# Linear attention and two mixture layers on one core: denominators on ScalarE, the first item in two single banks, numerators ahead of keys-values, and one decode step on GpSimd

## The chip, the cores and the metric

The kernel runs on one core of one Trainium2 chip. The metric is device time in microseconds (us), from the launch of the program to its end. Before the change it took 1583.85 us (median of 3 runs, 1583.15 to 1584.65).

The engines are named as the profile names them: PE is TensorE (PEld its weight loads, which overlap the matmuls), DVE is VectorE, ACT is ScalarE, POOL is GpSimd, SP is SyncE, which issues most DMAs. SBUF is the on-chip memory, PSUM the eight accumulator banks of 128 partitions x 512 fp32 that PE writes.

## The reference, cut to what matters

Three stages follow each other; the change lies in the first, and in the preparation of weights for the second.

```
# attention: q, k, v are (8, 8, 576, 64); w_phi is (64, 128)
proj = x @ w_phi;  proj -= max(abs(proj), axis=-1)
phi  = concat(exp(proj), exp(-proj))                    # 256 features, for q and for k
kv   = k_p^T v          (256 x 64 per head)
z    = sum over the sequence of k_p
num  = q_p @ kv;  den = q_p . z + 1e-6;  out = num / den
# second stage: h = x @ w_in; g = h * cos(h); g @ w_out      (4608 tokens, 512 -> 2048 -> 512)
# third stage: top-1 routing to 8 experts, relu MLP of each  (512 -> 1024 -> 512)
```

The weights of the second stage arrive as 64-bit floats and are decoded to fp32 on the chip.

## The kernel before, in words

**Attention** (`attention`, lines 46 to 326) works on 16 items, each a pair of batches and a pair of heads. An item has 9 blocks of 128 rows, in five groups `g` of 2, 2, 1, 2 and 2 blocks. `step(j,m)` (line 288) is one step of the steady state: it does one part of several items at once, so that the engines have independent work. An item of time is five steps, m = 0 to 4; m = 2 handles the group of one block and is about half as long. In a step, in this order:

- `proj` (line 151): PE multiplies the transposed q rows by `w_phi` into the PSUM tile `pj` and the transposed k rows into `pjk`. For each DVE then takes the maximum of the absolute values (L161) and subtracts it (L162), which gives `t_q` and `t_k`. So four DVE instructions a step.
- `outT` (line 250): PE transposes the finished rows `xs` of an earlier group into a free half of `pjk`, and ACT copies them to `xo` (L258).
- `qexp` (line 211): PE transposes `t_q` into the PSUM tile `tr`, ACT takes two exponentials, of plus and minus (L225).
- `turn` (line 133): PE transposes raw rows of a later item, ACT copies them (L143, L147).
- `kv` (line 185): PE accumulates keys-values into the PSUM tile `kv`, from the k exponentials `ke`; `kvfin` (line 204) copies the finished sums to SBUF on ACT (L208).
- `num` (line 229): PE multiplies the q exponentials by these sums into the PSUM tile `pn`, whose last column of each block is the denominator. DVE adds 1e-6 (L245), takes the reciprocal (L246) and multiplies (L247), which gives `xs`. `pn` is one bank, so the next numerators wait until L247 has read it.
- `kexp` (line 176): ACT takes the two k exponentials (L181).

The first item has no item before it to hide behind. `begin(m)` (line 271) drives it: its transposes go whole (`whole`, line 128) into the two halves of the one PSUM tile `tr`, and its projections alternate between `pj` and `pjk`, q and k in the same tile, with `by_bank` (line 165) for the second group.

**The weight decode** (`begin`, `decodes`, `decode_part`, lines 449 to 488) turns one 128 x 512 weight block in seven instructions: an absolute value on ACT (L459), then on DVE a minimum (L460), a shift (L461) and two bit-wise merges (L462, L463), a copy on ACT (L464) and a subtraction (L465). 21 blocks are decoded beside the attention, one instruction or two in each step, between the steps; the other 11 in the first part of the second stage. DVE and ACT keep the order in which the program writes these instructions (`pinned`, `keep`), and so does PE in the attention. The driver is at lines 918 to 933.

**The second and third stage** (`moes`, line 387) follow. `route1` (line 625) copies token numbers into `rec` with a DVE instruction that the scheduler may place (L648).

Of the kernel before, what the change touches and what calls it, by code (L numbers as in the profile page):

```python
# [11 lines left out]
F32 = mybir.dt.float32  # L12
# [8 lines left out]
P = 128  # L21
# [24 lines left out]
def attention(tc, ctx, S, ident, q, k, v, w_phi, xt):  # L46
# [7 lines left out]
    pp=pctx.enter_context(tc.tile_pool(name="a_ps",bufs=1,space=PSUM))  # L54
    pk=ctx.enter_context(tc.tile_pool(name="a_kv",bufs=1,space=PSUM,side="right"))
    pj,pjk=(pp.tile([P,2,512],F32,tag=n,name=n) for n in ("pj","pjk"))
    tr=pk.tile([P,2,512],F32,tag="tr",name="tr")
    flat=itertools.count()

    w2=ap.tile([P,F],F32,name="w2",bufs=1)  # L60
    for i in range(2): tc.keep_in_program_order(nc.scalar.dma_start(w2[i*D:(i+1)*D,:],w_phi))
    nc.scalar.preload_act_table_set("natural_log_exp_and_others")

    items=[(bp,hp) for bp in range(4) for hp in range(4)]
    NI=len(items)
# [57 lines left out]
    def over(dst,c,src):  # L123

        for r in range(2): keep(nc.tensor.transpose(dst[:,r,c*H:(c+1)*H],src[r*H:(r+1)*H],ident[r*H:(r+1)*H,r*H:(r+1)*H]))
    def got(dst,a,c): return dst[:,:,a*H:c*H].rearrange("p r (c t) -> p c r t",t=H)
    def like(x): return x.rearrange("p (c r t) -> p c r t",r=2,t=H)
    def whole(srcs):

        pt=tr[:,next(flat)%2,:]  # L130
        for c,x in enumerate(srcs): keep(nc.tensor.transpose(pt[:,c*P:(c+1)*P],x,ident))
        return pt
    def turn(i,m,pt=None,base=0):
# [14 lines left out]
        return vec  # L148

    ts={}  # L150
    def proj(i,g,t,out,o=0):
        c0,n=GR[g]
        x=T[t,i]
        for c in range(n):
            for s in range(2):
                keep(nc.tensor.matmul(out[:,s,o+c*F:o+(c+1)*F],x[s*D:(s+1)*D,(c0+c)*P:(c0+c+1)*P],w2[s*D:(s+1)*D,:],start=True,stop=True))  # L156
        tt=ts[t,i,g]=S(t+"t",f"t_{t}_{i}_{g}")
        def vec():
            gg=out[:,:,o:o+n*F].rearrange("p s (c f) -> p s c f",f=F)
            m=ap.tile([P,4],F32,tag=t+"m",name=f"m_{t}_{i}_{g}")[:,:2*n].rearrange("p (s c) -> p s c",s=2)  # L160
            keep(nc.vector.tensor_reduce(m,gg,AX.X,ALU.max,apply_absolute_value=True))  # L161
            keep(nc.vector.tensor_tensor(tt[:,:n*256].rearrange("p (s c f) -> p s c f",s=2,f=F),gg,  # L162
                m.unsqueeze(3).to_broadcast([P,2,n,F]),ALU.subtract))
        return vec
    def by_bank(i,g,out):
        ms=[]
        for s in range(2):
            ms.append(ap.tile([P,4],F32,tag="qk"[s]+"m",name=f"m_{s}_{i}_{g}"))
            keep(nc.vector.tensor_reduce(ms[s],out[:,s,:].rearrange("p (c f) -> p c f",f=F),AX.X,ALU.max,apply_absolute_value=True))
        for o,t in ((0,"q"),(1,"k")):  # L170
            for s in range(2):
                keep(nc.vector.tensor_tensor(ts[t,i,g][:,s*256:(s+1)*256].rearrange("p (c f) -> p c f",f=F),out[:,s,o*256:(o+1)*256].rearrange("p (c f) -> p c f",f=F),
                    ms[s][:,2*o:2*o+2].unsqueeze(2).to_broadcast([P,2,F]),ALU.subtract))
# [37 lines left out]
    def qexp(i,g):  # L211

        n=GR[g][1]; tt=ts.pop(("q",i,g))
        srcs=[tt[:,(s*n+c)*F:(s*n+c+1)*F] for c in range(n) for s in range(2)]
        w=2*n*P
        x=ap.tile([P,1024],F32,tag="qx",name=f"qx_{i}_{g}",bufs=4)
        qx[i,g]=x[:,:2*w].rearrange("p (k h c) -> p k h c",h=2,k=2)
        if i==0 and g<3:
            pt=whole(srcs)
            made=[(x[:,kk*w:(kk+1)*w],pt[:,:w]) for kk in range(2)]  # L220
        else:
            for c,y in enumerate(srcs): over(tr,4+c,y)
            made=[(like(x[:,kk*w:(kk+1)*w]),got(tr,4,4+2*n)) for kk in range(2)]
        def vec():
            for (o,p),sign in zip(made,(1.0,-1.0)): keep(nc.scalar.activation(o,p,AF.Exp,scale=sign))  # L225
        return vec

    xss={}; xos={}
    def num(i,g):

        n=GR[g][1]; t0=GR[g][0]
        x=qx.pop((i,g))
        pn=pk.tile([P,512],F32,tag="pn",name=f"pn_{i}_{g}")
        for t in range(n):
            for h in range(2):
                o=pn[:,(2*t+h)*E1:(2*t+h+1)*E1]
                for sg in range(2):
                    for c in range(2):
                        bb=c if t0+t==4 else int(t0+t>4)
                        keep(nc.tensor.matmul(o[64*c:64*c+64],x[:,sg,h,t*P+64*c:t*P+64*c+64],kvs[i,bb][:,2*h+sg,:],start=sg==0,stop=sg==1,skip_group_check=True))  # L240
        pv=pn[:,:2*n*E1].rearrange("p (g d) -> p g d",d=E1)
        xs=xss[i,g]=ap.tile([P,256],F32,tag="xs",name=f"xs_{i}_{g}",bufs=2)
        def vec():
            r=ap.tile([P,4,1],F32,tag="rd",name=f"rd_{i}_{g}")[:,:2*n,:]
            keep(nc.vector.tensor_scalar(r,pv[:,:,D:E1],1e-6,None,op0=ALU.add))  # L245
            keep(nc.vector.reciprocal(r,r))  # L246
            keep(nc.vector.tensor_tensor(xs[:,:n*P].rearrange("p (g d) -> p g d",d=D),pv[:,:,0:D],r.to_broadcast([P,2*n,D]),ALU.mult))  # L247
        return vec

    def outT(i,g):  # L250

        t0,n=GR[g]
        if g==0: xos[i]=ap.tile([P,9*P],F32,tag="xo",name=f"xo_{i}")
        xo=xos[i]; xs=xss.pop((i,g))
        po,base=(pjk,4) if (i,g)<(NI-1,0) else (tr,2*(g%2))
        for t in range(n): over(po,base+t,xs[:,t*P:(t+1)*P])
        def vec():
            keep(nc.scalar.copy(like(xo[:,t0*P:(t0+n)*P]),got(po,base,base+n)))  # L258
# [12 lines left out]
    def begin(m):  # L271

        for i,n in FIRST[m]: turn(i,n)()
        if m>1:
            kexp(0,m-2); qexp(0,m-2)()
        loads(0,m)
        yield
        if m==4: vecs=[proj(0,m,"q",pj),proj(0,m,"k",pjk)]
        else:
            out=(pj,pjk)[m%2]  # L280
            vecs=[proj(0,m,"q",out),proj(0,m,"k",out,256)]
            if m==1: vecs=[lambda: by_bank(0,m,out)]
        if m<1: warm(3)
        if m>1: kv(0,m-2)
        for f in vecs: f()
        if m==4: kvfin(0,0)
        yield
    def step(j,m):

        vecs=[]; dve=[]  # L290
        i,g=at(j,m-2); oi,og=at(j-1,m-2); ki,kg=at(j,m-1)
        if j<NI: dve.append(proj(j,m,"q",pj))
        if oi>=0: vecs.append(outT(oi,og))
        if j<NI: dve.append(proj(j,m,"k",pjk))
        two=j==1 and m==0
        if two: vecs+=[lambda: kexp(0,3),turn(2,0,pjk,4)]
        if i<NI: last=qexp(i,g)
        if two: vecs.append(turn(1,4,tr))
        elif j+1<NI: vecs.append(turn(j+1,m,tr))
        if i<NI: vecs.append(last)  # L300
        for f in vecs+dve: f()
        loads(j,m)
        yield
        if i<NI: kv(i,g)
        last=num(j-1,m)
        if i<NI and g in (2,4): kvfin(i,g//4)
        if ki<NI: kexp(ki,kg)
        last()
        if j==NI-1 and m==4: pctx.close()
        if j==NI and m==1: keep(nc.scalar.preload_act_table(AF.Sin))  # L310
        yield
# [75 lines left out]
def moes(tc, ctx, consts, S, ident, att, end_att, xt, w_in, w_out, x1d, tab, wgt, w1, w2, out):  # L387
# [61 lines left out]
    def begin():  # L449
# [7 lines left out]
        h,l=pair(wtag[which][f],f"w{which}_{f}")  # L457
        (win,wout)[which][f]=(h,l)
        return [lambda: pinned(nc.scalar.activation(t,H.bitcast(F32),AF.Abs,scale=2.0**-112)),  # L459
            lambda: pinned(nc.vector.tensor_scalar(t,t,F32_MAX,None,op0=ALU.min)),  # L460
            lambda: pinned(nc.vector.tensor_scalar(ti,ti,3,None,op0=ALU.logical_shift_left)),  # L461
            lambda: pinned(nc.vector.scalar_tensor_tensor(ti,L,29,ti,op0=ALU.logical_shift_right,op1=ALU.bitwise_or)),  # L462
            lambda: pinned(nc.vector.scalar_tensor_tensor(ti,H,-0x80000000,ti,op0=ALU.bitwise_and,op1=ALU.bitwise_or)),  # L463
# [1 line left out]
            lambda eng: eng.tensor_tensor(l,t,f32(h),ALU.subtract)]  # L465
    def decodes(n):

        d=begin(); yield d[0]()
        for k in range(n):
            d[1](); yield d[2]()  # L470
            yield d[3]()
            d[4](); old=d
            if k+1<n:
                d=begin(); d[0]()
            yield
            pinned(old[5]()); stage(); old[6](nc.gpsimd)
# [148 lines left out]
    def route1(u):  # L625
# [496 lines left out]
```

## Time and profile before

| | us |
|---|---|
| median of 3 runs | 1583.85 |
| the profiled execution | 1583.64 |
| its span, first to last instruction | 1581.9 |
| PE busy in it | 1550.4 (98%) |
| DVE busy in it | 1113.6 (70%) |
| ACT busy in it | 880.6 (56%) |
| POOL busy in it | 397.0 (25%) |

The span has two parts with different limits. The attention takes about the first 320 us; the second stage follows without a gap, then the third. The clock that the throttle granted to PE is at full speed throughout (the page's row PEclk shows 9, 90% or more, in each slice). Row DVE of the page's 40 slices shows 9 in the slices of the attention and 5 to 7 behind it.

### The profile page before, as it was taken

To read this page: it belongs to the slowest core of one execution; us is meant where nothing else is said; L and a number is where in the kernel's file an instruction comes from. 1 tells how busy PE (TensorE), PEld (TensorE's weight loads), DVE (VectorE), ACT (ScalarE), POOL (GpSimd) and SP (SyncE) were. 2 spreads that over 40 slices of the span, in tenths; PEclk is the share of its full clock that TensorE was granted. 3 is DMA by queue.
4 is the path that set the end of the run, shared out by engine and by line. 5 is a ranking of instruction groups with operands and counts; after the bars stand their busy time and mean duration, and the time that the engine had idled before them with its cause. 6 is when DMAs were issued, how large, how long until landed. Compare 5 with 4: busy or idle time off the path is not lost.

```text
span 1581.9 us, 35508 instructions
## 1 busy us (share of the span) xinstructions
PE 1550.4 (98%) x14065; PEld 1339.4 (85%) x14065; DVE 1113.6 (70%) x2303; ACT 880.6 (56%) x1627; POOL 397.0 (25%) x356
## 2 busy tenths in 40 slices
PE   8899999999999999999999999999999999999998
PEld 6889898878888888888888888888899899889986
DVE  6999999968657667675767677655776656565656
ACT  6788788766434344343534344344756656565656
POOL 1111110120223433333433433334122111211212
PEclk9999999999999999999999999999999999999999
DMA  7756555233200001010101001004748667766652
GB/s 213 210 159 172 157 167 156 94 111 95 92 14 24 25 13 41 14 40 8 40 14 41 14 9 39 8 15 152 257 147 323 228 225 255 247 227 220 239 197 86
DMA packets 140850, 189.33 MB, mean 120 GB/s; under 512 B 63015, under 2 KB 87719, under 8 KB 140674
## 3 DMA queue, kind: packets, MB, share of 16 engines
q1 hardware_dynamic: 132754, 166.11, 33.6%
q0 software_dynamic: 7760, 20.79, 3.8%
q8 instruction: 113, 1.85, 0.5%
q14 instruction: 63, 0.52, 0.1%
q10 hardware_dynamic: 160, 0.07, 0.0%
HBM read 155.88 MB, written 31.82 MB: 119 GB/s over the span
## 4 chain that ended last, share of the span: by engine, by line
PE 82%; DVE 12%; DMA 4%; issue 2%; ACT 0%; SPq 0%; POOLq 0%; DVEq 0%
PE ph L517 25%; PE acc L557 19%; PE mh L825 12%; PE po L837 11%; PE acc L562 6%; DMA xg<-x1d,mrec 2%; PE kv L201 2%; DVE t_q L162 2%; DVE t_k L162 2%; DVE m_q L161 2%; DVE m_k L161 2%; PE pn L240 2%; DVE xs L247 1%; PE pjk L156 1%; PE px L807 1%
## 5 line engine op out<-in xcount | busy, mean ns | idle before, releaser
L517 PE MATMUL ph<-x,w 128*128 128x512 f32 x1728 | 418.6, 391 | 2.2 <-DVE fr L539 1.6
L517 PEld LDWEIGHTS ph<-x,w 128*128 128x128 f32 x1728 | 322.7, 188 | 70.3 <-DVE fr L539 2.0
L546 POOL TENSOR_TENSOR gl<-fr,gh 128x512 fp32r<-128x512 f32 x130 | 194.8, 1501 | 433.5 <-DVE gh L545 386.1
L780 DVE TENSOR_TENSOR m<-raw,m 128x512 fp32r<-128x512 f32 x320 | 208.2, 687 | 101.1 <-ACT m L779 73.6
L557 PE MATMUL acc<-w,gh 128*128 128x512 f32 x896 | 275.8, 389 | 0.0
L530 ACT ACTIVATE n<-ph 128x512 int32<-128x512 f32 x144 | 86.0, 597 | 272.5 <-PE ph L517 272.4
L779 ACT CAST m<-raw 128x512 fp32r<-128x512 f32 x320 | 188.1, 619 | 39.5 <-PE mh L825 32.4
L825 PE MATMUL mh<-xT,m 128*128 128x256 f32 x1728 | 201.0, 277 | 0.0
L532 DVE SCALAR_TENSOR_TENSOR fr<-ph,n 128x512 f32<-128x512 f32 x144 | 99.2, 689 | 141.9 <-ACT n L530 127.9
L825 PEld LDWEIGHTS mh<-xT,m 128*128 128x128 f32 x1728 | 197.7, 188 | 1.1 <-DVE m L780 0.8
L557 PEld LDWEIGHTS acc<-w,gh 128*128 128x128 f32 x896 | 168.2, 188 | 34.9
L837 PE MATMUL po<-m,hh 128*128 128x512 f32 x576 | 179.6, 393 | 0.0
L593 DVE SCALAR_TENSOR_TENSOR junk<-x1T,wg 128x512 f32<-128x512 f32 x224 | 179.4, 801 | 0.0
L557 PE MATMUL acc<-w,gl 128*128 128x512 f32 x448 | 174.3, 389 | 0.0
L535 ACT ACTIVATE fr<-fr 128x512 f32<-128x512 f32 x144 | 91.1, 633 | 118.1 <-DVE fr L532 118.0
L539 DVE SCALAR_TENSOR_TENSOR fr<-fr,ph 128x512 f32<-128x512 f32 x144 | 98.7, 685 | 79.7 <-ACT fr L537 79.6
L837 PEld LDWEIGHTS po<-m,hh 128*128 128x128 f32 x576 | 105.2, 188 | 19.7
L837 PE MATMUL po<-m,hl 128*128 128x512 f32 x288 | 112.4, 390 | 0.0
L886 POOL DMA_INDIRECT out_dram<-o,mrec x38 | 43.3, 1139 | 266.2 <-ACT o L885 251.9
L557 PEld LDWEIGHTS acc<-w,gl 128*128 128x128 f32 x448 | 84.1, 188 | 17.5
L201 PE MATMUL kv<-v,ke 128*64 128x65 f32 x2560 | 93.3, 225 | 0.9 <-issue 0.9
L537 ACT ACTIVATE fr<-fr 128x512 f32<-128x512 f32 x143 | 90.4, 632 | 4.3
(244 smaller groups left out, 2262.3 us busy)
## 6 DMA issues: line engine op xcount, KB each, us to landing
raw<-in_moe_w_dram SPq DMA_DIRECT2D x160, 512.0 KB, 5.8
xt<-xo SPq DMA_DIRECT2D x16, 576.0 KB, 3.7
xr<-xt SPq DMA_DIRECT2D x36, 256.0 KB, 2.9
raw_q<-in_q_dram SPq DMA_DIRECT2D x32, 256.0 KB, 4.2
raw_k<-in_k_dram SPq DMA_DIRECT2D x32, 256.0 KB, 3.8
st<-in_moe_w_in_dram SPq DMA_DIRECT2D x16, 512.0 KB, 4.2
st<-in_moe_w_out_dram SPq DMA_DIRECT2D x16, 512.0 KB, 3.7
v<-in_v_dram SPq DMA_DIRECT2D x62, 128.0 KB, 4.5
```

The source lines that it names most:

```text
L201: keep(nc.tensor.matmul(o[f0:f0+64],e[:,col+f0:col+f0+64],vh[:,h,9 if cc==4 and bb else cc,:],start=start,stop=cc==(4,8)[bb],skip_group_ch ...
L517: nc.tensor.matmul(ph,A[:,ws],xhl[u,d][k],start=n[0]==0,stop=n[0]==11); n[0]+=1
L532: ins=nc.vector.scalar_tensor_tensor(g,ph,INV2PI,n,op0=ALU.mult,op1=ALU.subtract)
L539: out0[0]=nc.vector.scalar_tensor_tensor(g,g,-0.5,ph,op0=ALU.add,op1=ALU.mult)
L546: nc.gpsimd.tensor_tensor(gl,g,f32(gh),ALU.subtract)
L557: nc.tensor.matmul(accs[u][c],A[:,ws],B,start=(f==0 and k==0),stop=(f==NF-1 and k==2))
L562: nc.tensor.matmul(accs[u][d],A[:,ws],B,start=(f==0 and k==0),stop=(f==NF-1 and k==2))
L593: return lambda: tc.keep_in_program_order(nc.vector.scalar_tensor_tensor(junk,x1T[u,c],1.0,wg[e],op0=ALU.mult,op1=ALU.mult,accum_out=lgs[u ...
L779: keep(nc.scalar.copy(h,a))
L780: keep(nc.vector.tensor_tensor(l,a,f32(h),ALU.subtract))
L825: nc.tensor.matmul(ph[:,f2*T:(f2+1)*T],A[:,ws],B[d//2][:,xs],start=n==0,stop=n==11); n+=1
L837: nc.tensor.matmul(po[c],A[:,ws],B,start=(f==0 and j==0),stop=(f==NF2-1 and j==2))
```

## The change

Five edits, all of them in the attention and in the decode:

- The first item's whole transposes and its q exponentials use two tiles of one bank each, in a pool of their own (`a_first`), which is closed after `begin`; the tile `tr` of the steady state is made only then. Its projections go q into `pj` and k into `pjk`, as in the steady state; `by_bank` is gone.
- The addition of 1e-6 to the denominators is an ACT instruction (an identity with a bias from the small SBUF tile `eps`), and writes `rd` from PSUM to SBUF. It stands between the two q exponentials of a step, which are now issued separately (`half(0)`, `half(1)`).
- In a step `num` stands ahead of `kv`, and `kvfin` behind the k exponentials.
- The decode's minimum is a GpSimd instruction; DVE begins with the shift.
- The copy of token numbers in `route1` keeps its place in the program. One more group of the last-but-one item's output goes through `tr`.

```
+    first=ExitStack()
+    ps=first.enter_context(tc.tile_pool(name="a_first",bufs=2,space=PSUM,side="right"))
+    tr=[]
...
+    eps=ap.tile([P,1],F32,name="eps",bufs=1)
+    nc.gpsimd.memset(eps,1e-6)
...
-        pt=tr[:,next(flat)%2,:]
+        pt=ps.tile([P,512],F32,tag="tr",name="flat")
...
-        def vec():
-            for (o,p),sign in zip(made,(1.0,-1.0)): keep(nc.scalar.activation(o,p,AF.Exp,scale=sign))
-        return vec
+        def half(kk): keep(nc.scalar.activation(*made[kk],AF.Exp,scale=(1.0,-1.0)[kk]))
+        return half
...
+        r=ap.tile([P,4,1],F32,tag="rd",name=f"rd_{i}_{g}")[:,:2*n,:]
+        keep(nc.scalar.activation(r,pv[:,:,D:E1],AF.Identity,bias=eps))
         def vec():
-            r=ap.tile([P,4,1],F32,tag="rd",name=f"rd_{i}_{g}")[:,:2*n,:]
-            keep(nc.vector.tensor_scalar(r,pv[:,:,D:E1],1e-6,None,op0=ALU.add))
             keep(nc.vector.reciprocal(r,r))
...
-        po,base=(pjk,4) if (i,g)<(NI-1,0) else (tr,2*(g%2))
+        po,base=(pjk,4) if (i,g)<(NI-2,3) else (tr[0],2*(g%2))
...
     def begin(m):
         for i,n in FIRST[m]: turn(i,n)()
         if m>1:
-            kexp(0,m-2); qexp(0,m-2)()
+            half=qexp(0,m-2)
+            kexp(0,m-2); half(0); half(1)
         loads(0,m)
         yield
-        if m==4: vecs=[proj(0,m,"q",pj),proj(0,m,"k",pjk)]
-        else:
-            out=(pj,pjk)[m%2]
-            vecs=[proj(0,m,"q",out),proj(0,m,"k",out,256)]
-            if m==1: vecs=[lambda: by_bank(0,m,out)]
+        vecs=[proj(0,m,"q",pj),proj(0,m,"k",pjk)]
...
     def step(j,m):
...
-        if i<NI: kv(i,g)
         last=num(j-1,m)
-        if i<NI and g in (2,4): kvfin(i,g//4)
+        if i<NI: half(1)
         if ki<NI: kexp(ki,kg)
+        if i<NI:
+            kv(i,g)
+            if g in (2,4): kvfin(i,g//4)
         last()
...
     for m in range(5): yield from begin(m)
+    first.close()
+    pt=ctx.enter_context(tc.tile_pool(name="a_tr",bufs=1,space=PSUM,side="right"))
+    tr.append(pt.tile([P,2,512],F32,tag="tr",name="tr"))
...
-            lambda: pinned(nc.vector.tensor_scalar(t,t,F32_MAX,None,op0=ALU.min)),
+            lambda: nc.gpsimd.tensor_scalar(t,t,F32_MAX,None,op0=ALU.min),
...
     def decodes(n):
-        d=begin(); yield d[0]()
+        d=begin(); d[0](); yield d[1]()
         for k in range(n):
-            d[1](); yield d[2]()
+            yield d[2]()
             yield d[3]()
             d[4](); old=d
             if k+1<n:
-                d=begin(); d[0]()
+                d=begin(); d[0](); d[1]()
...
-        parts.append([lambda: (d[0](),d[1](),d[2]()), lambda: (d[3](),d[4](),d[5](),stage()), lambda: pinned(d[6](nc.vector))])
+        parts.append([lambda: (d[0](),d[1]()), lambda: (d[2](),d[3](),d[4](),d[5](),stage()), lambda: pinned(d[6](nc.vector))])
...
-        nc.vector.tensor_copy(rec[:,:,0],C["tok"].rearrange("p a c -> p (a c)")[:,4*u:4*u+4])
+        pinned(nc.vector.tensor_copy(rec[:,:,0],C["tok"].rearrange("p a c -> p (a c)")[:,4*u:4*u+4]))
```

The line numbers of the changed kernel differ: L156 becomes L159, L162 L165, L201 L194, L208 L201, L225 L217, L181 L174, L240 L232, L246 L238, L258 L250, and the new instructions are L236 (denominators on ACT) and L454 (minimum on GpSimd).

**PE in a steady step.** On PE, in a step of the third item, these rows stood (before): projections, transposes of `xs`, of `t_q` and of raw rows, then keys-values, then numerators.

```order
L156 MATMUL pj<-w_90,qT_607 128x128 x4
L125 MATMUL pjk<-ident,xs_1_1036 128x64 x4
L156 MATMUL pjk<-w_90,kT_402 128x128 x4
L125 MATMUL tr<-ident,t_q_1_953 128x64 x8
L125 MATMUL tr<-ident,raw_q_536 128x64 x8
L201 MATMUL kv_0_1098<-v_623,ke_1_1125 64x65 x16
L240 MATMUL pn_3_1211<-kvz_1_1037,qx_3_859 64x65 x16
```

The same place on PE in the changed kernel:

```order
L159 MATMUL pj<-w_92,qT_626 128x128 x4
L128 MATMUL pjk<-ident,xs_1_1038 128x64 x4
L159 MATMUL pjk<-w_92,kT_421 128x128 x4
L128 MATMUL tr<-ident,t_q_1_972 128x64 x8
L128 MATMUL tr<-ident,raw_q_555 128x64 x8
L232 MATMUL pn_3_1214<-kvz_1_1061,qx_3_879 64x65 x16
L194 MATMUL kv_0_1132<-v_641,ke_1_1129 64x65 x16
```

The last two groups have changed places; nothing else of the step has moved on PE.

**ACT in the step before and in this one.** On ACT the rows from the output copy of the half step on were (before):

```order
L258 COPY xo_1055<-pjk 128x256
L147 COPY kT_868<-tr 128x128
L147 COPY qT_1072<-tr 128x128
L225 ACTIVATE qx_0_1063<-tr 128x512 x2
L181 ACTIVATE ke_1_1125<-t_k_1_962 128x4x128 x2
L459 ACTIVATE d_t_2_1147<-st_0_842 128x512
L464 CAST w_1_757<-d_t_1_756 128x512
```

And in the changed kernel, with the last two rows of the step before them, where the copy `kvz` stands:

```order
L174 ACTIVATE ke_0_1042<-t_k_0_878 128x4x128 x2
L201 COPY kvz_1_1061<-kv_1_930 128x260
L250 COPY xo_1074<-pjk 128x256
L150 COPY kT_888<-tr 128x128
L150 COPY qT_1091<-tr 128x128
L217 ACTIVATE qx_0_1082<-tr 128x512
L236 ACTIVATE rd_2_1126<-pn_2_1116,eps 128x2
L217 ACTIVATE qx_0_1082<-tr 128x512
L174 ACTIVATE ke_1_1129<-t_k_1_981 128x4x128 x2
L453 ACTIVATE d_t_2_1166<-st_0_862 128x512
L458 CAST w_1_776<-d_t_1_775 128x512
```

The denominators `rd` stand between the two exponentials of `qx` and read `pn`, so ACT waits there for PE's numerators of the same step; the copy `kvz` stands behind the `ke` exponentials.

**PE in the first item.** On PE, rows of the second and third group of the first item (before):

```order
L131 MATMUL tr<-ident,raw_k_96 128x128 x4
L156 MATMUL pjk<-w_90,qT_115 128x128 x4
L156 MATMUL pjk<-w_90,kT_120 128x128 x4
L131 MATMUL tr<-ident,rl_k_97 128x128
L131 MATMUL tr<-ident,rl_q_99 128x128
L131 MATMUL tr<-ident,raw_q_98 128x128 x4
L131 MATMUL tr<-ident,t_q_0_154 128x128 x4
```

The same in the changed kernel:

```order
L134 MATMUL flat<-ident,raw_k_100 128x128 x4
L159 MATMUL pj<-w_92,qT_119 128x128 x4
L159 MATMUL pjk<-w_92,kT_125 128x128 x4
L134 MATMUL flat<-ident,rl_k_101 128x128
L134 MATMUL flat<-ident,rl_q_103 128x128
L134 MATMUL flat<-ident,raw_q_102 128x128 x4
L134 MATMUL flat<-ident,t_q_0_160 128x128 x4
```

The order is the same; the transposes write tiles named `flat` that are two in number in place of the one tile `tr`, and the projections of q and k are split over both tiles.

## Rows read from the trace of the kernel before

**Rows 1.** Windows: length, busy us and instructions of each engine, clock, DMA share, GB/s.
```profile
60.00:300.00 240.00, 229.01 (x5859) 215.34 (x5855) 223.68 (x505) 195.97 (x447) 28.27 (x53) 1.00 0.57 160
344.00:440.00 96.00, 96.00 (x427) 79.36 (x426) 69.71 (x121) 52.82 (x88) 13.33 (x9) 1.00 0.33 106
```

**Rows 2.** Timeline of SP (start, length, what): output of two items, ten apart.
```profile
72.74 0.38 SPq L261 DMA_DIRECT2D xt<-xo  x1
...
263.98 0.34 SPq L261 DMA_DIRECT2D xt<-xo  x1
```

**Rows 3.** Timeline of DVE in one full step.
```profile
182.59 0.68 DVE L161 TENSOR_REDUCE m_q<-pj 128x4 f32<-128x512 f32 x1
...
185.34 0.16 DVE L245 TENSOR_SCALAR rd<-pn 128x4 f32<-128x4 f32 x1
185.54 0.18 DVE L246 RECIPROCAL rd<-rd 128x4 f32<-128x4 f32 x1
...
186.10 0.68 DVE L463 SCALAR_TENSOR_TENSOR d_t<-st,d_t 128x512 int32<-128x512 int32 x1
186.69 0.68 DVE L161 TENSOR_REDUCE m_q<-pj 128x4 f32<-128x512 f32 x1
```

**Rows 4.** Timeline of DVE: start of a half step and of the next.
```profile
305.23 0.42 DVE L161 TENSOR_REDUCE m_q<-pj 128x2 f32<-128x256 f32 x1
...
307.40 0.68 DVE L161 TENSOR_REDUCE m_q<-pj 128x4 f32<-128x512 f32 x1
```

**Rows 5.** Groups of DVE, 60 to 314 us: count, busy us, mean ns, idle before.
```profile
L461 DVE TENSOR_SCALAR d_t<-d_t 128x512 int32<-128x512 int32 x18 | 7.7, 427 | 0.6
L460 DVE TENSOR_SCALAR d_t<-d_t 128x512 f32<-128x512 f32 x18 | 7.5, 416 | 0.0
```

**Rows 6.** Timeline of PE's weight loads in one full step.
```profile
185.23 0.52 PEld L156 LDWEIGHTS pj<-w,qT 64*128 64x128 f32 x8
...
186.98 1.01 PEld L201 LDWEIGHTS kv<-v,ke 128*64 128x64 f32 x32
187.91 1.02 PEld L240 LDWEIGHTS pn<-kvz,qx 128*64 128x64 f32 x32
189.00 0.19 PEld L156 LDWEIGHTS pj<-w,qT 64*128 64x128 f32 x2
```

**Rows 7.** Waits, 60 to 314 us: who waited for whom, total us, times, longest.
```profile
ACT xo L258 <- PE pjk L156: 38.8, 52, 1.8
PEld pjk L125 <- ACT ke L181: 13.4, 26, 0.9
...
DVE rd L245 <- PE pn L240: 7.0, 16, 1.0
...
PEld tr L125 <- issue: 1.3, 1, 1.3
```

**Rows 8.** Groups of ACT, 60 to 314 us, of two widths of one copy.
```profile
L258 ACT COPY xo<-pjk 128x256 f32<-128x256 f32 x53 | 19.9, 375 | 28.2 <-PE pjk L156 28.2
...
L258 ACT COPY xo<-pjk 128x128 f32<-128x128 f32 x14 | 3.7, 266 | 12.1 <-PE pjk L156 10.6 <-DVE d_t L460 1.5
```

**Rows 9.** Timeline of the first item: DVE, then PE's weight loads.
```profile
8.34 0.17 DVE L648 COPY rec<-tok 128x4 int32<-128x4 int32 x1 [3.41 <-POOL tok L351]
...
16.81 0.42 PEld L131 LDWEIGHTS tr<-ident,t_q 128*128 128x128 f32 x4 [0.91 <-ACT kT L143]
...
24.46 0.52 PEld L156 LDWEIGHTS pj<-w,qT 64*128 64x128 f32 x8 [0.59 <-DVE t_q L162]
```

**Rows 10.** Timeline of POOL and DVE, 316 to 321 us.
```profile
316.96 2.52 POOL L506 TENSOR_TENSOR x<-xr,x 128x512 fp32r<-128x512 f32 x2 [7.90 <-ACT x L505]
...
318.99 1.04 DVE L506 TENSOR_TENSOR x<-xr,x 128x512 fp32r<-128x512 f32 x1 [0.43 <-ACT x L505]
320.28 0.69 DVE L506 TENSOR_TENSOR x<-xr,x 128x512 fp32r<-128x512 f32 x1 [0.26 <-ACT x L505]
```

**Rows 11.** Groups of POOL, 0 to 420 us.
```profile
L465 POOL TENSOR_TENSOR w<-d_t,w 128x512 fp32r<-128x512 f32 x21 | 26.9, 1279 | 178.7 <-ACT w L464 178.7
```

More of the change, by code (lines that the diff above doesn't have):

```diff
@@ L56, in attention @@
     pj,pjk=(pp.tile([P,2,512],F32,tag=n,name=n) for n in ("pj","pjk"))
-    tr=pk.tile([P,2,512],F32,tag="tr",name="tr")
-    flat=itertools.count()
+    first=ExitStack()
+    ps=first.enter_context(tc.tile_pool(name="a_first",bufs=2,space=PSUM,side="right"))
+    tr=[]
     w2=ap.tile([P,F],F32,name="w2",bufs=1)
@@ L150, in attention, with proj @@
     ts={}
-    def proj(i,g,t,out,o=0):
+    def proj(i,g,t,out):
         c0,n=GR[g]
@@ L155, in proj @@
             for s in range(2):
-                keep(nc.tensor.matmul(out[:,s,o+c*F:o+(c+1)*F],x[s*D:(s+1)*D,(c0+c)*P:(c0+c+1)*P],w2[s*D:(s+1)*D,:],start=True,stop=True))
+                keep(nc.tensor.matmul(out[:,s,c*F:(c+1)*F],x[s*D:(s+1)*D,(c0+c)*P:(c0+c+1)*P],w2[s*D:(s+1)*D,:],start=True,stop=True))
         tt=ts[t,i,g]=S(t+"t",f"t_{t}_{i}_{g}")
         def vec():
-            gg=out[:,:,o:o+n*F].rearrange("p s (c f) -> p s c f",f=F)
+            gg=out[:,:,:n*F].rearrange("p s (c f) -> p s c f",f=F)
             m=ap.tile([P,4],F32,tag=t+"m",name=f"m_{t}_{i}_{g}")[:,:2*n].rearrange("p (s c) -> p s c",s=2)
@@ L164, in proj @@
         return vec
[L165 to L173, printed above, removed]
     es={}
@@ L221, in qexp @@
         else:
-            for c,y in enumerate(srcs): over(tr,4+c,y)
-            made=[(like(x[:,kk*w:(kk+1)*w]),got(tr,4,4+2*n)) for kk in range(2)]
-        def vec():
-            for (o,p),sign in zip(made,(1.0,-1.0)): keep(nc.scalar.activation(o,p,AF.Exp,scale=sign))
-        return vec
+            for c,y in enumerate(srcs): over(tr[0],4+c,y)
+            made=[(like(x[:,kk*w:(kk+1)*w]),got(tr[0],4,4+2*n)) for kk in range(2)]
+        def half(kk): keep(nc.scalar.activation(*made[kk],AF.Exp,scale=(1.0,-1.0)[kk]))
+        return half
     xss={}; xos={}
@@ L296, in step @@
         if two: vecs+=[lambda: kexp(0,3),turn(2,0,pjk,4)]
[L297 to L300, printed above, removed]
+        if i<NI: half=qexp(i,g)
+        if two: vecs.append(turn(1,4,tr[0]))
+        elif j+1<NI: vecs.append(turn(j+1,m,tr[0]))
+        if i<NI: vecs.append(lambda: half(0))
         for f in vecs+dve: f()
```

## The prediction

> **What bounds the kernel now.** I read the windows first, by stretches with different work. Between 60 and 300 us, the steady state of the attention, DVE is busy 223.68 of 240 us (93%), PE 229.01 (95%), its weight loads 215.34 (90%), ACT 195.97 (82%); behind it, from 344 to 440 us, PE is busy every microsecond and DVE 73% [rows 1]. So a saving on DVE can only come out in the first 320 us; from there on PE sets the end, and what the attention saves is handed on whole.
>
> The period of an item comes from the output transfers: 11 of them, ten intervals, from 72.74 to 263.98, so 19.12 us an item [rows 2].
>
> Next the timeline of DVE in one full step. Its instructions stand end to end: from one step's first maximum (182.59) to the next (186.69) 4.10 us, of which the decode's merge takes 0.59 (186.10 to 186.69), so 3.51 without decode [rows 3]. A half step is 2.17 [rows 4]. An item has four full steps and a half one, 4 x 3.51 + 2.17 = 16.2. To this come decodes, 18 in 254 us [rows 5], 1.36 an item, each about 0.42 for the minimum, 0.43 for the shift and twice 0.59: 2.8. Together 19.0, against a period of 19.12: DVE is the bound.
>
> Then PE. In the step from 185.23 to 189.00 its weight loads show no wait: 3.77 us, of which keys-values take 0.93 (186.98 to 187.91) [rows 6]. Over an item all parts but keys-values come 4.5 times (four full groups and a half), keys-values five times (the half group feeds both sums): 4.5 x 2.84 + 5 x 0.93 = 17.4. PE is second, 1.7 below the period. Its waits say the same: 13.4 us in 254 are for room in `pjk`, 1.0 an item, because the transposes of `xs` and the k projections must wait until DVE has read that tile (the row names ACT, which is only what ended nearest) [rows 7]. ACT works 0.82 x 19.12 = 15.6 an item and spends its waits on PE (38.8 us) [rows 1, 7].
>
> The page on reading traces in the Trainium skill (Perfetto Trace Analysis, Identifying the Most-Contended Engine) says that the busy share of matmuls is a poor measure of PE's headroom and that of the weight loads a better one. By the matmul share (95%) an item could shrink to 18.2 at best; by the loads' (90%) to 17.2. The step worked out above, 17.4, sides with the rule.
>
> **The change, part by part.** The sum is made against the profiled execution, 1583.64 us, 0.2 under the median of the runs shown.
>
> *Denominators to ACT.* DVE loses one instruction a step: from its start to that of the reciprocal is 0.20 us (185.34 to 185.54) [rows 3], five an item: 1.0. ACT gains five. The trace has no ACT instruction of 4 columns. Two widths of one copy are 375 ns for 256 columns and 266 for 128 [rows 8]; the line through them gives 0.16 for 4, and 0.27 is the upper end. I take 0.2: 1.0 an item, so ACT goes to 16.6, still below PE. The added wait: ACT stops at `rd` until PE's numerators are through, and behind it stand the second q exponential and the two of k; the last are read by PE only in the next step. DVE's reciprocal now waits for ACT. Counted from PE's start of a step: numerators would begin at 1.75 (186.98, where keys-values began) and be through about 1.1 later, `rd` at about 3.1; DVE begins its maxima about 0.75 after PE's start and needs 2.75 (182.59 to 185.34), so it comes to the reciprocal at 3.5. The wait is covered, with 0.4 to spare.
>
> *Numerators ahead of keys-values.* This is what covers that wait: in the old order numerators came 0.93 later, and DVE waited for them 7.0 us in 254, 0.5 an item [rows 7]. The same PE instructions remain, so PE's 17.4 stands. Two things get later: `kvz` is copied behind the k exponentials, and in the half step the numerators that read it come earlier. By the same count `kvz` ends about 4.9 after the start of the step before, and these numerators could begin at 3.77 + 1.2. It just fits; a miss costs some tenths once an item.
>
> *Minimum to GpSimd.* DVE loses another 0.42 x 1.36 = 0.6 an item [rows 5]. GpSimd has no such row; its two-input subtraction of this size takes 1.28 [rows 11], so I bound the minimum by 0.43 (as on DVE) and 1.28 and take 1.2. The minimum is issued a step or more ahead of the shift that needs it, over 3.5 us, which hides either end; without that cover it would cost 1.28 x 21 = 27. The 11 decodes in the second stage lie under PE's full row there: nothing.
>
> So DVE falls by 1.6 an item to 17.4 at most, level with PE's 17.4, with ACT at 16.6. Three engines that near to each other, tied step by step, won't reach the floor. Before, the excess over the higher of the two floors was small with the second 1.6 away; I allow 0.8 for the tighter coupling and for stretches like PE's 1.3 us that no engine explains [rows 7]. Period 18.2, a saving of 0.9. It applies to the 15 items of the steady state: 13.8 (0.4 to 1.6 an item: 6 to 24).
>
> *The first item.* The whole transposes wait each time for ACT to empty the one tile, though they write its other half: 0.9 us before the transposes at 16.81, and there are six such waits until 24.46, when the first steady step begins [rows 9]. With two tiles each waits only for the read before last. Against this, projections no longer alternate and wait for DVE's subtraction. Followed by hand with the durations of these rows: the first keys-values begin as before (ACT takes its exponentials behind a copy that waits for PE), the second group gains about 1.4, the first steady step begins 2.7 earlier, bounded then by DVE. The copy `rec`, which held up DVE until 8.34 for token numbers [rows 9], is pinned away; alone it would give 1.5, but it lies beside the chain just followed. I take 2.5 (0 to 3).
>
> Where the attention runs into the second stage, 300 to 344 us, ACT gets five more small waits among its work: 0 (1 either way).
>
> Sum: 1583.64 - 13.8 - 2.5 = 1567.3, so 1567.
>
> **The rivals.**
> - *PE is the bound sooner.* The wait for `kvz` misses by half a microsecond once an item, or ACT, at 16.6 with a stop in the middle, comes late with the tile `tr`: period 18.7. 0.42 x 15 + 2.5 = 8.8, so 1575. For it: the fit of 4.9 to 4.97; against: ACT has slack behind each late step.
> - *GpSimd holds up DVE.* DVE's two-input subtraction took 1.04 beside GpSimd's of the same kind, and 0.69 alone [rows 10]. If each of the 21 new minima lengthens one merge (two inputs in SBUF) by that 0.35: 7 lost, 1574. Against it: minimum and merges of successive blocks are steps apart, and the other DVE work there reads PSUM. The Trainium skill has the rule (SBUF — State Buffer, Who interferes with whom): a DVE instruction with two SBUF inputs contends with a GpSimd instruction that reads SBUF, and the loser waits for the whole of it; by that rule the row of 1.04 is such a wait, cut by where it began.
> - *Nothing moves*: something else paces the items, as DMA (57% busy [rows 1]), or ACT's new work takes back what DVE gives: 1583.
> - *Slower: the reciprocal waits for ACT at each step.* ACT reaches `rd` late, because what it does ahead is late, and DVE, which reads `rd` in order, stops. The change saves DVE 1.6 / 5 = 0.32 a step, so it turns to a loss when that wait passes 0.32 on average. At 0.45 it is (0.45 - 0.32) x 75 steps = 10 more, less the first item's 2.5: 1591. For it: a new round trip over three engines each step. Against: 0.4 of room, and ACT's idle time.
>
> **How the numbers follow.** The forecast gets 0.67 (its own range 1560 to 1572), PE sooner 0.17, GpSimd 0.05, nothing 0.04, slower 0.07. The range for 8 in 10 takes in the floor of the sums (1583.64 - 24 - 3 = 1557) and the first two rivals, without the last two: 1558 to 1577. A measurement can tell 0.2%, 3 us, from no change; so faster is 0.88, the same 0.05, slower 0.07.
>
> **What would show it.** In the changed profile, 60 to 280 us: ten output intervals of about 182 us; DVE's share down to about 90%, PE's loads up to 94%, the waits of `pjk` transposes far below 13.4; `rd` on ACT near 0.2 us and no long wait of the reciprocal; the first steady step's projection near 22 us; the second and third stage as long as before. I am wrong if the reciprocal waits for ACT in most steps, if the period stays over 18.8, or if anything behind 344 us has changed by over 2 us.

## The result, and the profile after

The changed kernel takes 1567.42 us (median of 4 runs, 1566.42 to 1569.89), against 1583.5 before in the same runs: a ratio of 0.9901 (95% interval 0.9884 to 0.9919). A second measurement on another occasion gave 1567.79 and 0.9894 (0.9879 to 0.9909). The forecast was 1567. The number was right; as the experiments show, it came about in another way than the sum said.

The windows of the changed kernel, in the columns of [rows 1]:

```profile
60.00:280.00 220.00, 219.06 (x5660) 209.25 (x5660) 201.15 (x413) 199.00 (x495) 51.99 (x69) 0.99 0.62 174
60.00:300.00 240.00, 238.10 (x6153) 227.26 (x6153) 219.10 (x450) 215.82 (x536) 54.96 (x72) 0.99 0.58 164
344.00:440.00 96.00, 95.78 (x425) 78.87 (x424) 65.88 (x115) 49.35 (x83) 28.93 (x19) 1.00 0.23 75
```

Between 60 and 300 us PE's matmuls went from 229.01 of 240 us to 238.10, its weight loads from 90% to 95%, ACT from 82% to 90%; DVE fell from 93% to 91%. PE has almost no gap left: 1.90 of 240 us.

SP's timeline, the outputs that answer to those of [rows 2]:

```profile
69.93 0.34 SPq L253 DMA_DIRECT2D xt<-xo  x1
...
250.59 0.34 SPq L253 DMA_DIRECT2D xt<-xo  x1
```

Ten intervals of 18.07 us, before 19.12. So the first of these outputs comes 2.8 us earlier than before, the last 13.4. PE's first matmul of the second stage started at 321.13 before and starts at 303.56 now, 17.6 earlier. From there to the end it is 1261.1 us (1564.7 - 303.56), before 1260.8 (1581.9 - 321.13): all of the gain lies in the attention, and the rest hands it on.

One full step on DVE, to be laid beside [rows 3]:

```profile
187.92 0.68 DVE L164 TENSOR_REDUCE m_q<-pj 128x4 f32<-128x512 f32 x1
188.64 0.69 DVE L165 TENSOR_TENSOR t_q<-pj,m_q 128x512 f32<-128x512 f32 x1
189.25 0.68 DVE L164 TENSOR_REDUCE m_k<-pjk 128x4 f32<-128x512 f32 x1
189.96 0.69 DVE L165 TENSOR_TENSOR t_k<-pjk,m_k 128x512 f32<-128x512 f32 x1
190.57 0.17 DVE L238 RECIPROCAL rd<-rd 128x4 f32<-128x4 f32 x1
190.85 0.42 DVE L239 TENSOR_TENSOR xs<-pn,rd 128x256 f32<-128x256 f32 x1
191.19 0.68 DVE L457 SCALAR_TENSOR_TENSOR d_t<-st,d_t 128x512 int32<-128x512 int32 x1
191.79 0.69 DVE L164 TENSOR_REDUCE m_q<-pj 128x4 f32<-128x512 f32 x1
```

The step is 3.87 with the merge, where it was 4.10. The weight loads of PE's long step, the one in which keys-values take 48 loads in place of 32:

```profile
190.19 0.52 PEld L159 LDWEIGHTS pj<-w,qT 64*128 64x128 f32 x8
190.77 0.23 PEld L128 LDWEIGHTS pjk<-ident,xs 64*128 64x128 f32 x4
190.89 0.56 PEld L159 LDWEIGHTS pjk<-w,kT 64*128 64x128 f32 x8
...
192.06 1.01 PEld L232 LDWEIGHTS pn<-kvz,qx 128*64 128x64 f32 x32
192.99 1.48 PEld L194 LDWEIGHTS kv<-v,ke 128*64 128x64 f32 x48
194.54 0.52 PEld L159 LDWEIGHTS pj<-w,qT 64*128 64x128 f32 x8
```

4.35 us, and no wait that the view shows. PE's own work in this step is 3.77 [rows 6] and 0.46 more for 16 loads (1.48 - 1.02), 4.23; the 0.12 above that come up between the start of the projections and that of the numerators (1.87 here, 1.75 in [rows 6] to keys-values).

The five steps of an item, from one start of the q projections on PE to the next (means over 12 or 13 items between 60 and 300 us; m = 2 is the half step, m = 0 the long one; the last row has the 4.23 from above and for the others the shortest that recurs in these runs):

| | m = 0 | 1 | 2 | 3 | 4 | sum |
|---|---|---|---|---|---|---|
| before | 5.06 | 3.77 | 3.00 | 4.12 | 3.18 | 19.1 |
| after | 4.45 | 3.76 | 2.84 | 3.80 | 3.12 | 18.0 |
| PE's own work | 4.23 | 3.77 | 2.74 | 3.77 | 3.12 | 17.6 |

The gain comes out mostly in two of the five steps, m = 0 (0.61) and m = 3 (0.32); m = 2 adds 0.16. Step m = 1 never had anything to give, because PE filled it before as well.

The waits, 60 to 304 us, that answer to [rows 7]:

```profile
ACT xo L250 <- PE pjk L159: 14.4, 34, 0.9
ACT rd L236 <- PE pn L232: 5.9, 18, 1.1
...
PE pjk L128 <- DVE rd L238: 3.0, 3, 2.7
...
PEld pjk L128 <- issue: 1.5, 5, 0.3
DVE rd L238 <- ACT rd L236: 1.4, 1, 1.4
...
PEld pn L232 <- ACT kvz L201: 0.9, 1, 0.9
```

Of the 13.4 us in which the weight loads of PE's transposes waited for room in `pjk` 1.5 are left, and the 7.0 of DVE for numerators are gone. The new wait of the reciprocal for ACT stands there once, in 67 steps. Two new operations, from the groups of ACT (60 to 304 us) and of POOL (0 to 420 us):

```profile
L236 ACT ACTIVATE rd<-pn,eps 128x4 f32<-128x4 f32 x54 | 14.8, 274 | 6.0 <-PE pn L232 5.9
```

```profile
L454 POOL TENSOR_SCALAR d_t<-d_t 128x512 f32<-128x512 f32 x32 | 49.6, 1550 | 196.6 <-ACT d_t L453 192.5 <-DVE fr L526 4.0
```

### The profile page after: what moved, and what is told of

It reads as the page before. It is cut to its first block, busy times and chain, and to the rows that moved or that the text cites. A ratio compares the mean times of both kernels' runs of the same rounds, so it can differ in the third digit from the quotient of the medians.

```text
span 1564.7 us, 35515 instructions
## 1 busy us (share of the span) xinstructions
PE 1547.8 (99%) x14065; PEld 1341.6 (86%) x14065; DVE 1096.5 (70%) x2189; ACT 892.5 (57%) x1707; POOL 447.9 (29%) x389
## 4 chain that ended last, share of the span: by engine, by line
PE 84%; DVE 6%; DMA 5%; ACT 4%; issue 1%; POOL 0%; POOLq 0%; SPq 0%; DVEq 0%; ACTq 0%
PE ph L511 23%; PE acc L551 18%; PE mh L819 12%; PE po L831 11%; PE acc L556 6%; PE pn L232 3%; DMA out_dram<-o,mrec 3%; PE kv L194 3%; PE pj L159 2%; PE pjk L159 2%; PE tr L128 1%; PE px L801 1%; DVE t_k L165 1%; DVE m_k L164 1%; DVE t_q L165 1%
## 5 line engine op out<-in xcount | busy, mean ns | idle before, releaser
L587 DVE SCALAR_TENSOR_TENSOR junk<-x1T,wg 128x512 f32<-128x512 f32 x224 | 186.1, 831 | 0.0
L454 POOL TENSOR_SCALAR d_t<-d_t 128x512 f32<-128x512 f32 x32 | 49.6, 1550 | 196.6 <-ACT d_t L453 192.5
```

The costliest lines, as they stand in the source:

```text
L587: return lambda: tc.keep_in_program_order(nc.vector.scalar_tensor_tensor(junk,x1T[u,c],1.0,wg[e],op0=ALU.mult,op1=ALU.mult,accum_out=lgs[u ...
```

## The experiments

"Period" is the mean of ten output intervals as above, from the profiled execution; ratios are to the kernel before, measured beside the run.

| run | median, us | ratio (95%) | period |
|---|---|---|---|
| before | 1583.5 to 1584.45 | | 19.12 |
| after, first and second time | 1567.42, 1567.79 | 0.9901, 0.9894 | 18.07, 18.13 |
| `b_order`: before with the new order only | 1577.64 | 0.9954 (0.9940 to 0.9968) | 18.51 |
| `b_min`: before with the minimum on GpSimd only | 1580.46 | 0.9969 (0.9957 to 0.9981) | 18.96 |
| `u_order`: after, order undone | 1589.0 | 1.0034 (1.0022 to 1.0046) | 19.66 |
| `u_den`: after, 1e-6 on DVE again | 1568.05 | 0.9909 (0.9892 to 0.9926) | 18.26 |
| `u_min`: after, minimum on DVE again | 1571.64 | 0.9918 (0.9904 to 0.9931) | 18.45 |
| `u_first`: after, old first item | 1567.86 | 0.9894 (0.9879 to 0.9909) | 18.19 |
| `k_fin` | 1569.12 | 0.9900 (0.9884 to 0.9917) | 18.31 |
| `v_parts` | 1569.17 | 0.9900 (0.9885 to 0.9916) | 18.42 |
| `v_late` | 1568.59 | 0.9898 (0.9881 to 0.9914) | 18.10 |
| `p_halfnum` | 1556.37 | 0.9822 (0.9806 to 0.9838) | 17.57 |
| `d_norecip` | 1611.16 | 1.0158 (1.0136 to 1.0180) | 18.04 |

**Denominators back on DVE** (`u_den`).

```
-        keep(nc.scalar.activation(r,pv[:,:,D:E1],AF.Identity,bias=eps))
         def vec():
+            keep(nc.vector.tensor_scalar(r,pv[:,:,D:E1],1e-6,None,op0=ALU.add))
```

> The changed kernel with the addition of 1e-6 back on VectorE; everything else as changed. Theory 1 (the item's period is the highest of the engines' floors and some coupling): DVE's floor rises by five additions of 0.2, from 17.3 to 18.3 an item, over PE's 17.4; period 18.07 to 18.6 or 18.8, so 8 to 11 us slower than the changed kernel. Theory 2 (the new order of numerators and keys-values made the gain, which engine adds 1e-6 is nothing): 0 to 3 us slower.

Not slower beyond noise: 1568.05. The period of 18.26 holds one interval of 19.95, in which PE stopped for about two microseconds with no releaser shown; the other nine are 18.07, the changed kernel's own. Theory 1 falls here: DVE has 208.03 of 220 us to do instead of 201.15, and it costs nothing.

**The order undone** (`u_order`).

```
+        if i<NI: kv(i,g)
         last=num(j-1,m)
         if i<NI: half(1)
+        if i<NI and g in (2,4): kvfin(i,g//4)
         if ki<NI: kexp(ki,kg)
-        if i<NI:
-            kv(i,g)
-            if g in (2,4): kvfin(i,g//4)
         last()
```

> The changed kernel with keys-values ahead of numerators again and the copy kvz ahead of the k exponentials; the denominators stay on ScalarE. Theory 1: PE's and DVE's floors stay, but rd now comes 0.93 us later in each step while DVE has no more than 0.4 us to spare, so DVE waits for it about 0.5 in each step: 5 to 25 us slower than the changed kernel, with a long wait of the reciprocal in the trace. Rival (slack elsewhere takes the wait up): 0 to 2 us slower.

Over 20 us slower than the changed kernel and slower than the kernel before. Its waits, 60 to 304 us:

```profile
ACT rd L236 <- PE pn L232: 42.3, 55, 1.5
...
DVE rd L238 <- ACT rd L236: 16.2, 33, 1.1
PE pjk L128 <- DVE rd L238: 8.1, 16, 1.2
```

This is the round trip of the slower rival, on three engines: ACT waits for the numerators at the end of PE's step, DVE's reciprocal for ACT, PE's transposes of `xs` for DVE.

**The order alone** (`b_order`), put into the kernel before.

```
-        if i<NI: kv(i,g)
         last=num(j-1,m)
-        if i<NI and g in (2,4): kvfin(i,g//4)
         if ki<NI: kexp(ki,kg)
+        if i<NI:
+            kv(i,g)
+            if g in (2,4): kvfin(i,g//4)
```

> The kernel before with one edit: numerators ahead of keys-values, and the copy kvz behind the k exponentials. The addition of 1e-6, the minimum and the first item stay as before. Theory D (the prediction's ledger: DVE's work an item sets the period, and the change gains by taking work off it): DVE's 19.0 an item is untouched, so 1580 to 1584. Theory O (each step is a chain from PE's numerators over DVE's xs to PE's next transposes, which stops PE; 0.93 us of keys-values behind the numerators cover it, and this makes most of the gain): long steps fall from 5.06 to about 4.8 and those behind the half step from 4.12 to about 3.9, so 0.5 to 0.8 an item, 1571 to 1577.

0.61 of the 1.05 us an item come with the order, DVE's work being the same. DVE's wait for numerators, 7.0 us before [rows 7], is gone; from the waits of `b_order`, 60 to 304 us:

```profile
DVE rd L245 <- PE pn L240: 0.2, 1, 0.2
```

The time fell by 6.8, less than 0.61 x 15 = 9.2, and why is not shown: the profiled execution, at 1580.78 the slowest of its five, began its steady state 2.3 us later than before (26.80 against 24.46), with PE's first transposes taking 1.06 us in place of 0.60, and lost 2.3 behind the attention, both where nothing was edited. One step on DVE without decode, from its timeline:

```profile
104.68 0.69 DVE L162 TENSOR_TENSOR t_k<-pjk,m_k 128x512 f32<-128x512 f32 x1
105.29 0.15 DVE L245 TENSOR_SCALAR rd<-pn 128x4 f32<-128x4 f32 x1
...
106.03 0.68 DVE L161 TENSOR_REDUCE m_q<-pj 128x4 f32<-128x512 f32 x1
```

The subtraction is followed by the addition after 0.61 us. In the step of [rows 3] the subtraction began at 184.63:

```profile
184.63 0.69 DVE L162 TENSOR_TENSOR t_k<-pjk,m_k 128x512 f32<-128x512 f32 x1
```

The addition came at 185.34, 0.71 later: 0.10 of that step was a wait for numerators. Over all steps from 60 to 300 us, the distances of this pair exceed the shortest by 9.2 us in all before, 0.7 an item, and by 0.3 in `b_order`. The whole step here is 3.39 (102.64 to 106.03), not 3.51, so DVE's work is about 18.5 an item. DVE's waits in `b_order` add up to 0.9 us in 244, so that with its 18.51 it is DVE that sets the period there.

**The minimum alone and undone** (`b_min`, `u_min`).

```
-            lambda: pinned(nc.vector.tensor_scalar(t,t,F32_MAX,None,op0=ALU.min)),
+            lambda: nc.gpsimd.tensor_scalar(t,t,F32_MAX,None,op0=ALU.min),
...
```

> The kernel before with one edit: the decode's minimum on GpSimd, issued right behind the absolute value. Theory D: 0.57 less DVE work an item, 0.57 x 15 = 8.5, so about 1575. Theory O: the chain from step to step stays, and only steps with a minimum and a shift between become shorter: 1579 to 1582.

> The changed kernel with the decode's minimum back on VectorE. Theory 1: DVE's floor rises by 0.42 x 1.36 = 0.57 to 17.9 an item, over PE's 17.4; period 18.3 to 18.5, so 4 to 6 us slower than the changed kernel. Theory 2 (the order made the gain): 0 to 2 us slower. A third: GpSimd's 1.55 us minimum costs DVE something by contention, then it is not slower or even faster.

In the old order the minimum's move brings 4.0 us, in the new one about 4 as well (1571.64 against 1567.42 and 1567.79). By period it is 0.38 an item in the new order. `u_min`'s profiled run was the slowest of its five, 1577.93, but it lost its time ahead of the ten intervals: ACT stood 7.28 us for a weight block until 61.40, and the output of item 1 came at 75.30, 5.4 us later than in the changed kernel. The intervals themselves are even, 17.95 to 18.79. The minimum's place makes it count: a decode puts minimum and shift, merge and merge into three steps in a row, and in `u_min` DVE works without a gap from 177.01 to 189.64, while PE waits 0.76 in the long step. `b_min` fits theory O: DVE still waits for numerators there, longer than before, so part of what the minimum frees goes into that wait (60 to 304 us):

```profile
DVE rd L245 <- PE pn L240: 8.6, 19, 1.1
```

**The first item undone** (`u_first`): the first group of the change's diff taken back, the copy of token numbers left pinned.

```
-        vecs=[proj(0,m,"q",pj),proj(0,m,"k",pjk)]
+        if m==4: vecs=[proj(0,m,"q",pj),proj(0,m,"k",pjk)]
+        else:
+            out=(pj,pjk)[m%2]
+            vecs=[proj(0,m,"q",out),proj(0,m,"k",out,256)]
+            if m==1: vecs=[lambda: by_bank(0,m,out)]
...
```

> The changed kernel with the first item as before (one tile of two banks for the whole transposes, projections in turn in pj and pjk, one group by banks); the copy of token numbers stays pinned. Theory 1 (two single banks bring the gain of the first item): first steady projection about 24.4 in place of 21.41, 2.5 to 3 us slower than the changed kernel. Rival (pinning the copy of token numbers, which stood in DVE's way until 8.34, brought it): 0 to 1.5 us slower.

Both half right. The first steady projection of the changed kernel, on PE's weight loads, and that of `u_first`:

```profile
21.41 0.52 PEld L159 LDWEIGHTS pj<-w,qT 64*128 64x128 f32 x8 [0.60 <-DVE t_q L165]
```

```profile
25.02 0.52 PEld L158 LDWEIGHTS pj<-w,qT 64*128 64x128 f32 x8 [0.60 <-DVE t_q L164]
```

3.6 us apart, but the output of item 1 only 1.1 (69.93 against 71.02), and the median of the whole time not beyond noise (1567.86 against 1567.42 and 1567.79). ACT's timeline of the changed kernel, then SP's, show where it stays:

```profile
51.65 1.21 ACT L174 ACTIVATE ke<-t_k 128x512 f32<-128x512 f32 x2
56.75 0.66 ACT L453 ACTIVATE d_t<-st 128x512 f32<-128x512 f32 x1 [3.89 <-DMA st<-in_moe_w_in_dram]
```

```profile
50.48 0.60 SPq L1075 DMA_DIRECT2D x1d<-zero  x1
51.19 0.42 SPq L436 DMA_DIRECT2D st<-in_moe_w_in_dram  x1
```

The third weight block is issued at 51.19, behind SP's other transfers, as it was before (50.75); ACT, now earlier, wants it at 52.9 and stands 3.89 us, and behind it the exponentials and copies that PE needs. In `u_first` ACT takes the block at 56.18 without a wait.

**Taking that wait away** (`v_parts`, `v_late`).

```
-    PARTS={n:1 for n in range(11,165,2)}
-    PARTS.update({25:2,55:2,85:2,115:2,169:4})
+    PARTS={n:1 for n in range(11,165,2) if n!=25}                      # v_parts
+    PARTS.update({55:2,85:2,115:2,135:2,155:2,169:4})
```

```
-    PARTS.update({25:2,55:2,85:2,115:2,169:4})
+    PARTS.update({25:0,27:2,29:2,55:2,85:2,115:2,169:4})               # v_late
```

> The changed kernel with the decode's fifteenth-step pieces (n=25) put one step later and two pieces made up for at n=135 and 155, so that the third weight block is needed about 3.7 us later. In the changed kernel ScalarE waits 3.9 us there for that block's transfer, which is theory W's account of why the first item's 3.6 us come out only in small part. Theory W: this wait goes, 2 to 4 us faster than the changed kernel, 1563 to 1566. Rival (the steady state makes the loss up anyway, being bound by PE, or the wait turns up at another transfer): within 1 us of the changed kernel.

> The changed kernel with two pieces of the decode (n=25) put one step later (n=27) and one of n=27 to n=29, so that the third weight block is needed 3.7 us later, while all later pieces stand where they stood. Theory W: ScalarE's wait of 3.9 us for that block's transfer goes and 2 to 3.5 us come out: 1564 to 1566. Rival (the next transfers are late instead, or the steady state makes it up): within 1 us of the changed kernel.

Both miss theory W. `v_parts` loses the wait (0.56 is left) but moves every later decode piece up to n = 155 into another step, and its period rises to 18.42. `v_late` keeps them, and the wait turns up at the next block:

```profile
56.56 0.69 ACT L453 ACTIVATE d_t<-st 128x512 f32<-128x512 f32 x1
69.89 0.66 ACT L453 ACTIVATE d_t<-st 128x512 f32<-128x512 f32 x1 [4.43 <-DMA st<-in_moe_w_in_dram]
```

So a later use of one block alone gains nothing. That the arrival of weight blocks holds the early items is argued from these waits and not shown: an earlier issue was not tried.

**What sets the period now** (`p_halfnum` leaves out half of the numerators' matmuls, `d_norecip` the reciprocal).

```
-                for sg in range(2):
+                for sg in range(1):                                    # p_halfnum
...
```

```
-    nc.gpsimd.memset(eps,1e-6)
+    nc.gpsimd.memset(eps,1e-12)
...
-        keep(nc.scalar.activation(r,pv[:,:,D:E1],AF.Identity,bias=eps))
+        keep(nc.scalar.activation(r,pv[:,:,D:E1],AF.Identity,scale=0.0,bias=eps))
         def vec():
-            keep(nc.vector.reciprocal(r,r))                            # d_norecip
```

> The changed kernel without the second half of the numerators' matmuls (the features exp(-proj) are left out of numerators and denominators), so PE has 0.49 us less in a full step, 2.2 an item. If PE sets the changed kernel's period (18.07, against 17.6 for PE's own work by step): period 17.2 to 17.5, where DVE stands, 9 to 13 us faster than the changed kernel. If DVE still sets it: within 2 us.

> The changed kernel without VectorE's reciprocal (numerators are multiplied by a constant that ScalarE's instruction writes in the place of the denominators), so DVE has 0.27 us less in each step, 1.3 an item. If PE sets the changed kernel's period: 0 to 2 us faster than the changed kernel in the attention. If DVE's work still sets it, as the prediction's ledger has it: 8 to 12 us faster.

Less PE work: 11 us faster, period 17.57. Less DVE work: the period stays (18.04), and the second stage begins at 303.19 against 303.56. (Its total is longer behind 1100 us, where PE is busy 490 us in place of 459, with 3185 matmuls in place of 3056; the third stage routes rows by their values, which differ in this run.) The waits of `d_norecip`, 20 to 304 us, show DVE waiting for PE:

```profile
DVE m_q L164 <- PE pj L159: 13.5, 30, 1.3
```

With DVE's part of the chain from numerators to `xs` 0.27 shorter a step the period stands, so neither DVE's work nor that chain holds it; ACT has the same work in `p_halfnum`, where the period falls. PE sets the changed kernel's period. Of PE's 2.2 us an item `p_halfnum` gives back only 0.5, so another bound lies close below.

**The copy `kvz` earlier** (`k_fin`).

```
-        if ki<NI: kexp(ki,kg)
         if i<NI:
             kv(i,g)
             if g in (2,4): kvfin(i,g//4)
+        if ki<NI: kexp(ki,kg)
```

> The changed kernel with keys-values and the copy kvz ahead of the k exponentials on ScalarE (PE's order stays). The prediction held that kvz behind the exponentials just fits (4.9 against 4.97 us). If that copy is late now: 1 to 5 us faster. If it fits, and the exponentials' readers on PE, or keys-values that ScalarE must wait for, count for more: same or up to 10 us slower.

Not faster; the period is 18.31, and ACT now waits for keys-values (2.4 us in 244). The copy behind the exponentials does fit. The last run, `a_again`, is the changed kernel itself:

> The changed kernel once more, unaltered, as the measure for the other runs of this call: 1566 to 1570, ratio about 0.990.

## Why the prediction was right, and where its steps were not

**What bounds the kernel: half right.** DVE was the engine with the most to do, but its 19.0 us an item held waits. The step's 3.51 was read off starts that follow each other closely, and one distance of 0.71 hid a wait of 0.10. `b_order` shows 18.5. The remaining 0.6 of the 19.12 were the chain of the old order: numerators were PE's last work in a step, DVE made `xs` from them, and PE's next step needed `xs` and room in `pjk` after its first projections. Most of that stood in [rows 7] as DVE's 7.0 us, 0.5 an item, beside PE's 13.4; I named both and priced neither as a gain.

**Denominators to ACT: the step that failed.** It was booked as 1.0 us an item, the larger part of the saving; it brings nothing (`u_den`). With order and minimum in place PE sets the period, and DVE's spare time has no taker (`d_norecip`). With the minimum still on DVE the move shows no gain of its own by period either (`u_min` 18.45, `b_order` 18.51); by median `u_min` lies 6.0 us under `b_order`, but it has the new first item too, and the two were not taken apart. In the old order it would have done harm (`u_order` has 19.66, `b_min` 18.96). Its recorded duration is 0.27, the upper end that was named, but the instruction behind it starts 0.14 to 0.16 after it, so it holds ACT up for less than the 0.2 that was taken.

**Numerators ahead: mis-sized.** Booked as cover for the new wait and otherwise as nothing. The cover is real, one wait of 1.4 us in 67 steps; but the order is worth 0.61 an item by itself. The count that `kvz` just fits held: one wait of 0.9 us in 244, and `k_fin` gains nothing.

**Minimum to GpSimd: right in kind.** 0.6 an item booked; in the old order 0.16 by period, some 4 us in all in either order. Where the order has made DVE the bound, it pays more by period: `u_den`, which beyond `b_order` has the minimum's move and the first item, is at 18.07 without the interval of its stop, `b_order` at 18.41 without its longest: 0.34 less. The minimum takes 1.49 us on GpSimd in the attention, above both bounds (0.43 and 1.28), and the cover of over 3.5 us hides it. DVE's merges take 682 ns in the attention, before 680, so the rival of contention falls there, where the two hardly overlap. Behind 320 us they do, and six merges take 0.74 to 1.07 us, 1.4 more in all than at 0.68 each:

```profile
378.82 1.07 DVE L457 SCALAR_TENSOR_TENSOR d_t<-st,d_t 128x512 int32<-128x512 int32 x1
```

```profile
378.73 1.49 POOL L454 TENSOR_SCALAR d_t<-d_t 128x512 f32<-128x512 f32 x1 [3.25 <-ACT d_t L453]
```

So the rival's mechanism is real, under a row of PE that is full. This merge ended ahead of the minimum (379.89 against 380.22): it took 0.39 longer, whereas by the rule that the prediction cites it would have waited for the whole of the minimum.

**The period: right by luck.** 18.2 forecast, 18.07 measured. The saving was booked as 1.6 taken off DVE, less 0.7 for coupling; it came as 0.6 from the order, 0.3 to 0.4 from the minimum behind it, and nothing from the denominators. That the two sums come so near is compensation. The floor that holds is PE's: 17.6 by step (17.4 was booked), and 0.4 over it where 0.8 was allowed. The first rival had the right engine, but neither its reasons (a late `kvz`, a late `tr`) nor its 18.7.

The Trainium skill (Perfetto Trace Analysis, Identifying the Most-Contended Engine) says to optimize the engine with the highest occupancy first. Here the row of before gives that as DVE (93%, PE's weight loads 90%); the runs show that work taken from DVE paid 0.16 an item in the old order, and work merely reordered on PE 0.61, as it closed DVE's gaps. The next section of that page of the Trainium skill (Optimization Strategy), on finding the gaps and what blocks them, is what the waits of [rows 7] called for.

**The first item: the mechanism right, its worth not.** 2.5 us booked, 3.05 at the first steady projection against before. Nothing beyond noise is left of it at the end (`u_first`). What the trace shows is that the third weight block arrives no earlier: before, ACT took that block at 58.14; in the changed kernel it is ready for it 5 us sooner, and that is sooner than the block. With this block's wait gone (`v_late`) the next one waits. I had looked at no transfer there.

**Behind the attention:** nothing forecast, 0.4 us longer measured.

Order and minimum give 6.8 and 4.0 us alone, but all edits together about 16; by period 0.61 and 0.16 alone, 1.05 together. The traces give a reason for the 0.28 between: with the order in place DVE waits for nothing, so what is taken off it counts down to PE's floor; without it part goes into the wait for numerators (7.0 us before, 8.6 in `b_min`). This is argued: no run has order and minimum and nothing else.

What stays open: of the 17.6 us at the start of the second stage, 15 x 1.05 = 15.8 are the period, and the rest is not taken apart. The two smallest edits, the pinned copy and the extra group through `tr`, were not run alone. Single profiles carry 1 to 2 us of their own: PE's stop in `u_den`, and in the same place a long interval before (19.74) and in `b_order` (19.37), so a difference of 0.1 to 0.2 in a period says little.

## What to carry to other kernels

Where an engine's instructions stand end to end, compare the distance of each pair of starts with the same pair elsewhere before you add them up as work; a wait of 0.1 us a step hides there. Where three engines hand work round once a step, price the order on the engine that closes the loop first, and a load taken off an engine only up to the next engine's floor. When something is made to start earlier, look at the transfers it reads: here they did not move with it.

## What the hardware showed that was not expected

GpSimd's minimum with one input takes 1550 ns for 128x512 as the mean of all 32, and 1488 in the attention, longer than its subtraction with two inputs (1277 ns in the same run) and 3.6 times DVE's 416. ACT's read of 128x4 from PSUM is recorded with 274 ns and that of 128x2 with 308, as much as its copy of 128x128 (265): below 128 columns these durations show no further fall, where I had drawn the line on to 0.16. They overlap the next instruction, though, which starts 0.14 to 0.16 us after the read of 128x4.
